# A packed attention followed by a squared-ReLU layer on one core: the first softmax in five token blocks instead of six, with a newly written order

## The chip, the core and the metric

The kernel runs on one core of a Trainium2 chip. The core has TensorE (PE; its weight loads are shown apart as PEld), VectorE (DVE), ScalarE (ACT), GpSimd (POOL) and SyncE (SP). Transfers are issued from POOL's, SP's and ACT's queues and are carried by 16 DMA engines. The metric is the time of one launch on the device, in microseconds (us). All other durations come from one profiled execution.

## The reference

Eight batches, eight heads, 576 tokens of 64 values, and 32 packing queries per head. Two attentions follow each other, and a two-layer network with a squared ReLU takes the result:

```python
def sm_attn(qq, kk, vv):
    s = scale * np.matmul(qq, kk.transpose(0, 1, 3, 2))
    s = s - np.max(s, axis=-1, keepdims=True)
    a = np.exp(s)
    a = a / (np.sum(a, axis=-1, keepdims=True) + 1e-09)
    return np.matmul(a, vv)
p_packed = sm_attn(p, k, v)              # 32 x 576 scores per head
out = sm_attn(q, p_packed, p_packed)     # 576 x 32 scores per head
x = out.transpose(0, 2, 1, 3).reshape(4608, 512)
h = np.maximum(x @ w_in, 0.0)            # w_in 512 x 2048
return (h * h) @ w_out                   # w_out 2048 x 512
```

## The kernel before

A batch is worked in two quads of four heads, so that 4 heads x 32 packing queries fill 128 partitions. Everything is done in bf16 with f32 accumulation; the POOL queue's loads cast on the way. The order of the work is a written string, `ORDER`, of some 2,000 words. Each word issues one step, each engine runs its own steps in the order of the words, and no scheduler moves them. A suffix names the engine: `:v` DVE, `:a` ACT, `:p` POOL; without one the engine is DVE. The digits after the letters are the batch and, where there is one, the quad. The words that matter here:

- `Lk`, `Lv`, `Lq`, `LA`, `LB`: loads of k and v (per quad), of q (per batch), and of the first 320 (A) and the other 256 (B) tokens of q in batches 0 and 1. `Wi` and `Wo` load pieces of w_in and w_out. They all go through POOL's one queue in the order of the words. `Pr`, `pg` load p, `Pu` makes a second copy of it with the partition halves swapped.
- First softmax: `kT` (DVE transposes k in 32x32 blocks, line 344), `s1` (scores, line 369), `m1` (maximum, line 393), `x1` (exponential on ACT, line 399), `eT` (PE transposes the result, line 412, in six blocks of 96 tokens), `eo` (copy out of PSUM), `pv` (times v, line 434: 6 blocks x 4 heads x 2 quads = 48 matmuls of 64 columns), `pp`, `bd`, `pt`, `po` (scaling and layouts of the packed result).
- Second softmax: `qT` or `qA`, `qB` (transposes of q, line 357), `s2` or `zA`, `zB` (scores), `t2`/`tA`/`tB`, `m2`/`mA`/`mB`, `sb`/`sA`/`sB`, `x2`/`xA`/`xB`, `su`/`uA`/`uB`, `a2`/`aA`/`aB` (back to rows, maximum, difference, exponential, sums, division) and `aT`/`TA`/`TB` (the result transposed, line 535).
- The packed result is multiplied with w_in first, so that the output of the second softmax needs no matmul of its own: `wa`, `wb`, `w0`, `w1` (line 546) and their copies `Wa`, `Wb`, `W0`, `W1` out of PSUM. `wa` and `wb` take the first half of the columns, in two parts; `w1` takes the second half.
- `h` (line 562) is the first layer: two matmuls for one of 16 blocks of 128 hidden columns and one part of the tokens. Blocks 0 to 3 and 8 to 11 need only `Wa` and `Wb`, the other eight need `W1`. `h0.0.*` are the 320 tokens of part A, `h0.1.*` the 256 of part B. `r` is the ReLU out of PSUM (ACT line 567, DVE line 569), `q` the square (lines 605, 607). Four PSUM banks take `h`, so an `h` waits for the `r` of four blocks before.
- `o` (line 618) is two of 16 matmuls of a tile of 128 output tokens, `c` its copy out of PSUM, `d` its store (line 639). The last tile is copied half by ACT (line 625) and half by DVE (line 626), and stored by two queues with two transfers each.
- `Z` (line 328) are idle matmuls that keep PE's clock up in the first 21 us.

## Time and profile before

| | us |
|---|---|
| median of three runs | 245.67 (244.76 to 246.89) |
| the profiled execution's own time | 245.67 |
| its span, first to last instruction | 243.9 |
| what lies around the span | 1.8 |
| PE busy | 231.7 |
| DVE busy | 205.9 |
| ACT busy | 142.4 |
| POOL busy | 69.3 |

The granted TensorE clock is 0.998 over the span. The profile's page gives the busy time of each engine, the span in 40 slices, the chain of work that ended last, and the costliest groups of instructions with their mean duration and the idle time before them. Durations in a group are those of one instruction; neighbours on PE overlap, so the pace of a group is read from the start of the first to the end of the last. "Idle before" with an arrow names what ended the wait.

### The profile page before, as it was taken

To read this page: it belongs to the slowest core of one execution; us is meant where nothing else is said; L and a number is where in the kernel's file an instruction comes from. 1 tells how busy PE (TensorE), PEld (TensorE's weight loads), DVE (VectorE), ACT (ScalarE), POOL (GpSimd) and SP (SyncE) were. 2 spreads that over 40 slices of the span, in tenths; PEclk is the share of its full clock that TensorE was granted. 3 is DMA by queue.
4 is the path that set the end of the run, shared out by engine and by line. 5 is a ranking of instruction groups with operands and counts; after the bars stand their busy time and mean duration, and the time that the engine had idled before them with its cause. 6 is when DMAs were issued, how large, how long until landed. Compare 5 with 4: busy or idle time off the path is not lost.

```text
span 243.9 us, 6139 instructions
## 1 busy us (share of the span) xinstructions
PE 231.7 (95%) x2424; PEld 128.8 (53%) x2460; DVE 205.9 (84%) x448; ACT 142.4 (58%) x315; POOL 69.3 (28%) x109
## 2 busy tenths in 40 slices
PE   8889899999999999999999999999999999999991
PEld 5556563455545655456445555565445554555540
DVE  3579987999989989798999999978898999677720
ACT  3418993577787859673666578644775667331200
POOL 8448832667690752072001800001000000000000
PEclk9999999999999999999999999999999999999999
DMA  6999999999999999456733991211332112121313
GB/s 152 198 197 209 203 207 200 143 192 273 161 193 212 168 154 217 86 74 115 111 73 82 121 173 27 63 43 46 50 90 59 36 38 46 43 60 28 86 43 86
DMA packets 34876, 29.00 MB, mean 119 GB/s; under 512 B 14112, under 2 KB 29856, under 8 KB 34848
## 3 DMA queue, kind: packets, MB, share of 16 engines
q0 software_dynamic: 28048, 18.26, 53.5%
q1 hardware_dynamic: 6640, 10.23, 16.0%
q8 instruction: 19, 0.31, 0.5%
q10 hardware_dynamic: 160, 0.13, 0.2%
q14 instruction: 9, 0.07, 0.1%
HBM read 37.22 MB, written 9.44 MB: 191 GB/s over the span
## 4 chain that ended last, share of the span: by engine, by line
PE 80%; DVE 9%; DMA 5%; issue 2%; POOL 1%; ACT 1%; POOLq 0%; ACTq 0%
PE ps_o L618 47%; PE ps_h L562 24%; DMA q_b<-in_q_dram 4%; PE ps_wp L546 3%; PE ps_s L369 3%; PE ps_e1T L412 2%; PE ps_pv L434 1%; DVE mx L500 1%; DVE gT L607 1%; DMA out_dram<-o_sb 1%; DVE sums L518 1%; DVE qT L357 1%; DVE r L569 1%; DVE s L495 1%; DVE s L492 1%
## 5 line engine op out<-in xcount | busy, mean ns | idle before, releaser
L618 PE MATMUL ps_o<-w_out_bf,gT 128*128 128x512 bf16 x540 | 145.1, 379 | 3.1 <-issue 1.7
L567 ACT ACTIVATE r<-ps_h 128x288 bf16<-128x288 f32 (+2 forms) x177 | 68.2, 417 | 51.9 <-PE ps_h L562 50.2
L562 PE MATMUL ps_h<-a2T,wp 128*128 128x288 bf16 (+2 forms) x512 | 91.2, 286 | 0.9 <-DVE wp L407 0.6
L618 PEld LDWEIGHTS <-gT 128*128 128x128 bf16 x576 | 53.7, 98 | 41.3 <-issue 5.5
L562 PEld LDWEIGHTS <-wp 128*128 128x128 bf16 x512 | 48.4, 98 | 44.1 <-issue 5.0
L607 DVE TENSOR_TENSOR gT<-r 128x576 bf16<-128x576 bf16 (+2 forms) x110 | 47.1, 445 | 2.6 <-ACT r L567 1.6
L569 DVE TENSOR_SCALAR r<-ps_h 128x288 bf16<-128x288 f32 (+2 forms) x79 | 34.9, 450 | 9.5 <-PE ps_h L562 8.9
L264 POOL DMA_DIRECT2D k_b<-in_k_dram x27 | 17.7, 656 | 47.3 <-DVE kT L344 37.2
L405 ACT CAST wp<-ps_wp 128x1024 bf16<-128x1024 f32 (+1 forms) x25 | 23.4, 953 | 6.1 <-PE ps_wp L546 6.1
L289 POOL DMA_DIRECT2D v_b<-in_v_dram x16 | 11.1, 697 | 39.8 <-PE ps_pv L434 38.0
L405 ACT COPY o_sb<-ps_o 128x512 f32<-128x512 f32 x25 | 14.5, 589 | 7.8 <-PE ps_o L618 7.6
L344 DVE STREAM_TRANSPOSE kT<-k_b 128x576 uint32<-128x576 uint32 x16 | 15.1, 950 | 2.4 <-DMA k_b<-in_k_dram 1.6
L399 ACT ACTIVATE e<-ps_s,nm 128x576 bf16<-128x576 f32 x16 | 11.8, 746 | 6.6 <-DVE nm L393 6.5
L328 PE MATMUL ps_idle<-gT 128*128 128x288 bf16 x92 | 14.5, 309 | 1.1 <-DVE gT L187 1.1
L512 ACT ACTIVATE e<-d 128x576 f32<-128x576 f32 (+2 forms) x20 | 11.4, 592 | 5.8 <-POOL d L506 4.0
L357 DVE STREAM_TRANSPOSE qT<-q_b 128x576 uint32<-128x576 uint32 (+2 forms) x20 | 12.2, 636 | 1.8 <-DMA q_b<-in_q_dram 1.6
L266 POOL DMA_DIRECT2D k_b<-in_k_dram x19 | 11.7, 617 | 3.8 <-DMA w_out_bf<-in_moe_w_out_dram 2.0
L407 DVE CAST wp<-ps_wp 128x1024 bf16<-128x1024 f32 x9 | 11.0, 1221 | 1.6 <-PE ps_wp L546 1.6
L518 DVE TENSOR_REDUCE sums<-e 128x18 f32<-128x576 f32 (+2 forms) x20 | 12.2, 612 | 0.0
L526 DVE TENSOR_TENSOR a<-e,rs 128x576 bf16<-128x576 f32 (+2 forms) x18 | 12.0, 680 | 0.0
L264 POOL DMA_DIRECT2D q_b<-in_q_dram x16 | 10.9, 684 | 3.3 <-DVE qT L357 2.3
L393 DVE TENSOR_REDUCE nm<-ps_s 128x1 f32<-128x576 f32 x16 | 11.6, 739 | 0.2 <-PE ps_s L369 0.2
(54 smaller groups left out, 179.2 us busy)
## 6 DMA issues: line engine op xcount, KB each, us to landing
out_dram<-o_sb SPq DMA_DIRECT2D x70, 128.0 KB, 2.4
v_b<-in_v_dram POOLq DMA_DIRECT2D x16, 288.0 KB, 7.4
w_out_bf<-in_moe_w_out_dram POOLq DMA_DIRECT2D x4, 512.0 KB, 12.5
q_b<-in_q_dram POOLq DMA_DIRECT2D x6, 288.0 KB, 7.5
q_b<-in_q_dram POOLq DMA_DIRECT2D x12, 144.0 KB, 7.5
k_b<-in_k_dram POOLq DMA_DIRECT2D x12, 108.0 KB, 4.5
w_in_bf<-in_moe_w_in_dram POOLq DMA_DIRECT2D x4, 256.0 KB, 11.3
w_in_bf<-in_moe_w_in_dram POOLq DMA_DIRECT2D x2, 512.0 KB, 13.0
```

The lines of the kernel that those rows point to most:

```text
L264: engine.dma_start(x[n:], s[:P - n])
L328: self.nc.tensor.matmul(ps[:, :HALF], lhsT=self.nought[:, :P], rhs=self.nought, start=True, stop=True)
L344: return self.nc.vector.transpose(t["kT"][:].rearrange("p (j l a) e -> p a j l e", j=J, a=3).bitcast(U32).rearrange("p a j l e -> p a j (l ...
L357: self.nc.vector.transpose(out.bitcast(U32), x.bitcast(U32))
L405: engine.copy(out, x)
L518: nc.vector.reduce_sum(out=sums[:, x], in_=t["e2"][:, x], axis=AX.X)
L526: engine.tensor_tensor(out=a2[:, y].rearrange("p t i e -> p t e i"), in0=t["e2"][:, x].rearrange("p (t e) i -> p t e i", e=2), in1=t["rs"] ...
L562: self.nc.tensor.matmul(ps, lhsT=t["wp"][:, fb // n, fb % n * P:(fb % n + 1) * P], rhs=t["a2T"][:, s0:s1], start=(qd == 0), stop=(qd == se ...
L567: engine.activation(r, ps, ACT.Relu)
L569: engine.tensor_scalar_max(r, ps, 0.0)
L607: engine.tensor_tensor(out=out, in0=r, in1=r, op=ALU.mult)
L618: self.nc.tensor.matmul(self.o[tt], lhsT=self.gT[:, fb, a:a + P], rhs=self.w_out_bf[:, fb, :], start=(i == 0), stop=(i == self.NFB - 1))
```

## The change

Five edits and a new order:

- From batch 2 on, the first softmax is transposed in four blocks of 128 tokens (every fourth token, so the weights of the transpose are read at a step of 4 elements) and a fifth block that holds the last 128 tokens again, of which v has the first 64 rows set to zero. So `eT` has 5 transposes for 6 and `pv` 40 matmuls for 48. Batches 0 and 1 keep six blocks of 96, read at a step of 6.
- v goes to static tiles: in batches 0 and 1 into parts of the big tile `gT` that are not yet used, from batch 2 into three tiles in turn, with two transfers for each instead of one.
- The keys are transposed in token order, so that `kT` writes without a step, and k comes in runs of nine tokens instead of three from batch 2. The exponential puts the columns in order instead: it writes each row of bf16 at a step of 18 elements.
- The last output tile is copied into two tiles, each stored by one transfer; the tokens of its block are laid out so that each transfer takes 128 rows. The last `aT` becomes two transposes.
- The second p load is issued from ACT's queue, not SP's; `Pu` is two copies by an engine, not two transfers.
- `ORDER` is another one from the start to the end. Idle matmuls: 90 instead of 92.

The start of the order is shown, and every changed function; the rest of `ORDER` is cut.

```diff
 NP = 32
-J = 6
 T = 18
-PS = 96
-S = J * PS
+S = T * NP
 HALF = S // 2
...
+THREES = range(2)
+
 PIECES = range(2)
...
 ORDER = """
-Lk00 I pf Lk01 Lv00 LB0 Lv01 kc:v kc:a LA0 pg P0 Wi11 kT00 Wi01 Wi00 kT01 Z32 s100 Wi10 Z1 s101 m100 Wi21 m101 x100
-x101 qB01 Wi20 Z10 eT00 qB00 eo00:a Z1 eT01 rd0 eo01:v Lk10 Z4 pv0 pp0 Z4 pt0 bd0 Lk11 qA01 po0:a zB0 qA00 tB00 Z2 zA0
-P1 tA01 tA00 mA01 mA00 sA01:p mB00 Lv10 sA00:v xA01 tB01 xA00 sB00:p uA01 Z23 wa01 wa00 Wo0 uA00 Wa00:a Wa01:a aA01:v
-mB01 xB00 aA00:p Z8 wb01 wb00 TA01 Wb01:a Lv11 sB01:v Wb00:a TA00 uB00 xB01 Z7 h0.0.0 h0.0.2 uB01 r0.0.0:a aB00:p
-h0.0.3 h0.0.9 r0.0.2:a Wo2 h0.0.8 aB01:v h0.0.10 r0.0.3:a TB00 r0.0.9:v r0.0.8:a h0.0.1 TB01 h0.0.11 q0.0.4:a
-r0.0.10:v h0.1.2 q0.0.1:p r0.0.1:v h0.1.8 r0.0.11:a r0.1.2:v h0.1.1 q0.0.0:a r0.1.8:v h0.1.9 h0.1.0 r0.1.9:a LA1
-q0.0.5:v w101 r0.1.1:a w100 q0.1.4:v W101:a h0.1.10 W100:v h0.1.3 h0.1.11 LB1 r0.1.0:a r0.1.3:a kT10 q0.1.0:p h0.0.12
-r0.1.10:a r0.1.11:a h0.1.7 h0.1.14 q0.1.1:a r0.0.12:v h0.0.13 Wo1 r0.1.14:a kT11 h0.1.12 r0.1.7:a h0.0.4 q0.1.5:a
+Lk00 I pf Lk01 Lv00 Lv01 LA0 kc:v kc:a Wi01 P0 kT00 Wi00 LB0 Z30 s100 Wi10 kT01 Wi11 m100 Z4 s101 Wi21 m101 x100 x101
+Wi20 Z15 eT00 rd0 eT01 eo00:v pg eo01:v Lk10 qA01 Z5 pv0 qA00 pp0 Lk11 Z4 pt0 bd0 zA0 po0:v tA01 tA00 Z4 wa01 mA01
+Wa01:a Z1 wa00 mA00 Wa00:a sA01:p qB01 Wo0 sA00:v xA01 qB00 xA00 uA01 Lv10 Z13 zB0 uA00 aA01:p tB00 Lv11 aA00:v Z8
+wb00 mB00 Wb00:a TA01 sB00:p TA00 tB01 Z6 h0.0.9 P1 h0.0.8 xB00 h0.0.0 mB01 r0.0.8:a uB00 wb01 sB01:p r0.0.0:a h0.0.1
+Wb01:a r0.0.9:v LA1 xB01 r0.0.1:v h0.0.10 aB00:p q0.0.4:a h0.0.3 uB01 h0.0.2 h0.0.11 q0.0.0:v r0.0.10:a r0.0.3:a
+r0.0.2:v aB01:p r0.0.11:a TB00 q0.0.1:v w100 Wo2 w101 TB01 W100:a q0.0.5:v h0.1.8 h0.1.9 W101:v h0.1.1 r0.1.9:a h0.1.0
+LB1 r0.1.8:a h0.1.3 r0.1.0:a h0.1.2 q0.1.4:v r0.1.1:a h0.0.4 r0.1.3:a kT10 q0.1.0:p h0.0.5 r0.1.2:a h0.0.13 r0.0.4:a
+kT11 h0.0.6 r0.0.5:a h0.0.12 Wo1 r0.0.13:a q0.1.1:v h0.0.7 r0.0.6:a q0.0.2:v s11 r0.0.12:a Wo3 h0.1.4 r0.0.7:v
+q0.0.6:a h0.1.15 m110 h0.1.12 q0.0.3:p r0.1.4:a h0.0.15 r0.1.12:a h0.1.14 r0.1.15:v r0.0.15:a h0.1.6 m111 h0.1.13
...
 """
...
         self.att, self.den, self.r, self.o, self.o_sb, self.ph = {}, {}, {}, {}, {}, {}
-        self.stage, self.open = -1, {}
+        self.stage, self.open, self.loaded_v = -1, {}, 0
         self.engines = {"v": self.nc.vector, "a": self.nc.scalar, "p": self.nc.gpsimd}
...
         nc.vector.memset(self.nought, 0.0)
+
+        self.v_b = [self.consts.tile([P, QH, 5, D], BF16, name=f"v_b{i}") for i in range(3)]
+        for x in self.v_b:
+            nc.vector.memset(x[:P // 2, :, 4, :], 0.0)
...
             self.load_rows(self.p_f[:, self.NQ + qd, :],
-                           self.p[1, qd * QH:qd * QH + QH].rearrange("h i d -> (h i) d"), qd, self.nc.sync)
+                           self.p[1, qd * QH:qd * QH + QH].rearrange("h i d -> (h i) d"), qd, self.nc.scalar)
...
-    def p_rest(self, word):
+    def p_rest(self, word, engine):
...
         else:
-            self.nc.sync.dma_start(z[P // 2:], y[:P // 2])
-            self.nc.sync.dma_start(z[:P // 2], y[P // 2:])
+            self.copy(engine, z[P // 2:], y[:P // 2])
+            self.copy(engine, z[:P // 2], y[P // 2:])
...
         if n == "v":
-            x = t[n] = self.ld.tile([PS, QH, J, D], BF16, name="v_b")
-            self.nc.gpsimd.dma_start(x, s.rearrange("h (p j) d -> p h j d", j=J))
+            self.load_v(t, s, b, qd)
             return
         x = t[n] = self.ld.tile([P, T, D], BF16, name="k_b")
+        s = s.rearrange("h (l t) d -> (h l) t d", t=T)
         if b == 0 and qd == 0:
-            self.nc.sync.dma_start(self.k_f, s.rearrange("h (l t) d -> (h l) (t d)", t=T))
+            self.nc.sync.dma_start(self.k_f, s.rearrange("p t d -> p (t d)"))
+        elif b in WIDE:
+            for hf, y in enumerate(WIDE_CUTS):
+                self.load_rows(x[:, y, :], s[:, y, :], qd + 2 * hf)
+        else:
+            self.load_rows(x, s, qd if b else 0)
+
+    def load_v(self, t, s, b, qd):
+
+        if b in THREES:
+            c = b * S
+            x = self.gT[:, self.NFB - 2 - 2 * b - qd, c:c + QH * 6 * D].rearrange("p (h j d) -> p h j d", h=QH, d=D)[:S // 6]
+            t["v"] = [x[:, :, j, :] for j in range(6)]
+            self.nc.gpsimd.dma_start(x, s.rearrange("h (p j) d -> p h j d", j=6))
             return
-        s = s.rearrange("h (l t) d -> (h l) t d", t=T)
-        if b in WIDE:
-            for hf in range(2):
-                y = slice(hf * J // 2, (hf + 1) * J // 2)
-                self.load_rows(*(z.rearrange("p (a j) d -> p a j d", j=J)[:, :, y, :] for z in (x[:], s)), qd + 2 * hf)
-        else:
-            self.load_rows(x, s, qd if b else 0)
+        x = self.v_b[self.loaded_v % len(self.v_b)]
+        self.loaded_v += 1
+        t["v"] = [x[:, :, j, :] for j in range(5)]
+        self.nc.gpsimd.dma_start(x[:, :, :4, :], s[:, :4 * P].rearrange("h (p j) d -> p h j d", j=4))
+        self.nc.gpsimd.dma_start(x[P // 2:, :, 4, :], s[:, 4 * P:].rearrange("h p d -> p h d"))
...
         t["kT"] = self.tp.tile([P, S, 2], BF16, name="kT")
-        return self.nc.vector.transpose(
-            t["kT"][:].rearrange("p (j l a) e -> p a j l e", j=J, a=3).bitcast(U32).rearrange("p a j l e -> p a j (l e)"),
-            t["k"][:].rearrange("p (a j) d -> p a j d", j=J).bitcast(U32))
+        self.nc.vector.transpose(t["kT"][:].rearrange("p s e -> p (s e)").bitcast(U32),
+                                 t["k"][:].rearrange("p t d -> p (t d)").bitcast(U32))
...
             self.den[b] = self.sm.tile([P, 2], F32, name="den")
-        self.nc.scalar.activation(e1[:].rearrange("p (a s) -> p a s", a=2), t["ps_s1"][:, :, :HALF], ACT.Exp,
+        self.nc.scalar.activation(e1[:].rearrange("p (l a u) -> p a u l", a=2, u=T // 2),
+                                  t["ps_s1"][:, :, :HALF].rearrange("p a (u l) -> p a u l", l=NP), ACT.Exp,
                                   bias=t["nm"], accum_out=self.den[b][:, qd:qd + 1])
...
     def st_e1T(self, t, b):
-        ps = self.bank16(b, "ps_e1T")[:PS, :J * P].rearrange("p (j c) -> p j c", c=P)
-        for j in range(J):
-            self.nc.tensor.transpose(ps[:, j, :], t["e1"][:, j * PS:(j + 1) * PS], self.ident)
+
+        m = 6 if b in THREES else 4
+        n = S // m // NP
+        n = min(n, QH)
+        x = [t["e1"][:, j:n * m * NP:m] for j in range(m)]
+        if n * m < T:
+            x.append(t["e1"][:, S - P:])
+        ps = self.bank16(b, "ps_e1T")[:n * NP, :len(x) * P].rearrange("p (j c) -> p j c", c=P)
+        for j, y in enumerate(x):
+            self.nc.tensor.transpose(ps[:, j, :], y, self.ident)
         t["ps_e1T"] = ps
     def st_e1T_out(self, t, engine):
-        t["e1T"] = self.tp.tile([PS, J, P], BF16, name="e1T")
-        self.copy(engine, t["e1T"], t["ps_e1T"])
+        ps = t["ps_e1T"]
+        t["e1T"] = self.tp.tile([P, T // 3, P], BF16, name="e1T")[:ps.shape[0], :ps.shape[1], :]
+        self.copy(engine, t["e1T"], ps)
...
         n = len(qds)
-        for j, i in [(j, i) for j in range(J) for i in range(n)] if b else [(j, i) for i in range(n) for j in range(J)]:
+        m = range(len(self.att[b, qds[0]]["v"]))
+        for j, i in [(j, i) for j in m for i in range(n)] if b else [(j, i) for i in range(n) for j in m]:
             t = self.att[b, qds[i]]
...
                 self.nc.tensor.matmul(ps[g:g + NP, i, :D], lhsT=t["e1T"][:, j, g:g + NP],
-                                      rhs=t["v"][:, h, j, :], start=(j == 0), stop=(j == J - 1))
+                                      rhs=t["v"][j][:, h, :], start=(j == 0), stop=(j == m[-1]))
...
-    def st_a2T(self, t, hf=None):
+    def st_a2T(self, t, hf=None, last=False):
...
         a2T = self.new(t, self.keep, "a2T", [P, S], BF16)
-        self.nc.vector.transpose(a2T[:, x.start * NP:x.stop * NP].bitcast(U32),
-                                 t["a2"][:, x.start // 2:x.stop // 2].rearrange("p t i e -> p (t i e)").bitcast(U32))
+        y = slice(x.start // 2, x.stop // 2)
+        if last:
+            y = slice(y.start, y.stop - 2)
+            self.nc.vector.transpose(a2T[:, y.stop * 2 * NP:].bitcast(U32).rearrange("p (l t) -> p t l", t=2),
+                                     t["a2"][:, y.stop:].rearrange("p t i e -> p t (i e)").bitcast(U32))
+        self.nc.vector.transpose(a2T[:, y.start * 2 * NP:y.stop * 2 * NP].bitcast(U32),
+                                 t["a2"][:, y].rearrange("p t i e -> p (t i e)").bitcast(U32))
...
     def step_c(self, engine, tt):
-        o = self.o_sb[tt] = self.op.tile([P, self.NE], F32, name="o_sb")
         ps, h = self.o.pop(tt), self.NE // 2
         if tt == self.B * S // P - 1:
-            self.nc.scalar.copy(o[:, :h], ps[:, :h])
-            self.nc.vector.tensor_copy(o[:, h:], ps[:, h:])
-        else:
+            o = self.o_sb[tt] = [self.op.tile([P, self.NE], F32, name="o_sb")[:, :h] for _ in range(2)]
+            self.nc.scalar.copy(o[0], ps[:, :h])
+            self.nc.vector.tensor_copy(o[1], ps[:, h:])
+        else:
+            o = self.o_sb[tt] = self.op.tile([P, self.NE], F32, name="o_sb")
             self.copy(engine, o, ps)
     def step_d(self, engine, tt):
-        nc = self.nc
-        o, h = self.o_sb.pop(tt), self.NE // 2
-        for n in range(P // (2 * NP)):
-            bl, cc = divmod(tt * P + n * 2 * NP, S)
-            rows = self.out[bl * S:(bl + 1) * S, :].rearrange("(l t e) n -> t l e n", t=T // 2, e=2)[cc // (2 * NP)]
-            src = o[n * 2 * NP:(n + 1) * 2 * NP]
-            last = tt == self.B * S // P - 1
-            for eng, c in ((nc.scalar, slice(0, h)), (nc.sync, slice(h, 2 * h))) if last else ((nc.sync, slice(0, 2 * h)),):
-                eng.dma_start(rows[:, :, c], src[:, c])
+
+        o, h, m = self.o_sb.pop(tt), self.NE // 2, 2 * NP
+        rows = self.out.rearrange("(b l t e) n -> b t l e n", b=self.B, t=T // 2, e=2)
+        if tt == self.B * S // P - 1:
+            rows = self.out[-S:].rearrange("(l t) n -> l t n", t=T)[:, T - 4:]
+            self.nc.scalar.dma_start(rows[:, :, :h], o[0])
+            self.nc.sync.dma_start(rows[:, :, h:], o[1])
+            return
+        for n in range(2):
+            b, t = divmod(tt * 2 + n, T // 2)
+            self.nc.sync.dma_start(rows[b, t], o[n * m:n * m + m])
...
             "a2": lambda: self.st_a2(t, engine),
-            "aT": lambda: self.st_a2T(t),
+            "aT": lambda: self.st_a2T(t, last=b == self.B - 1),
             "tA": lambda: self.st_turn2(t, 0),
...
         elif word in ("Pr", "Px", "Pt", "Pu"):
-            self.p_rest(word)
+            self.p_rest(word, engine)
         elif word[:2] == "kc":
```

151 lines of the change are left out of this document (75 added, 76 removed).

## The prediction

> **What bounds the kernel now.** The page's busy times and its chain of work come first.
>
> ```profile
> PE 231.7 (95%) x2424; PEld 128.8 (53%) x2460; DVE 205.9 (84%) x448; ACT 142.4 (58%) x315; POOL 69.3 (28%) x109
> ...
> PE 80%; DVE 9%; DMA 5%; issue 2%; POOL 1%; ACT 1%; POOLq 0%; ACTq 0%
> ```
>
> PE holds four fifths of the chain. The table of windows (us, PE busy, PEld, DVE, ACT, POOL, PE's clock, DMA share, GB/s) tells where it is not busy:
>
> ```profile
> 25.00:30.00 5.00, 4.34 (x73) 2.48 (x70) 4.92 (x9) 5.00 (x15) 4.20 (x6) 1.00 1.23 202
> 30.00:35.00 5.00, 4.89 (x83) 3.16 (x73) 5.00 (x13) 4.91 (x14) 1.94 (x3) 1.00 1.26 207
> ...
> 120.00:130.00 10.00, 9.79 (x106) 4.43 (x101) 9.93 (x18) 6.90 (x16) 0.00 (x0) 1.00 0.24 54
> ```
>
> From about 36 to 239 us PE is full: the nineteen 10 us windows from 40 to 230 leave it 2.9 us idle in all. DVE is nearly as full (9.93 of 10), so the order keeps both. Between 25 and 35 us ACT and DVE are full and PE is not, and before 21.4 us PE does mostly idle matmuls. So an edit is worth what it takes from PE after 36 us, what it moves of the moment from which PE is full, and what it takes from the end. The timeline of the start, all engines:
>
> ```profile
> 14.38 0.91 DVE L357 STREAM_TRANSPOSE qT<-q_b 128x320 uint32<-128x320 uint32 x2 [0.82 <-DMA q_b<-in_q_dram]
> ...
> 21.44 4.02 PE L562 MATMUL ps_h<-a2T,wp 128*128 128x320 bf16 x26
> ...
> 23.53 0.29 DVE L535 STREAM_TRANSPOSE a2T<-a 128x128 uint32<-128x128 uint32 x1
> ...
> 25.40 0.63 PE L546 MATMUL ps_wp<-w_in_bf,ppT 64*32 64x512 bf16 x16
> ...
> 27.40 2.10 PE L562 MATMUL ps_h<-a2T,wp 128*128 128x320 bf16 x14 [0.61 <-DVE wp L407]
> ...
> 33.44 0.50 PE L412 MATMUL ps_e1T<-ident,e 128*96 128x128 bf16 x6
> ...
> 34.73 0.56 PE L434 MATMUL ps_pv<-v_b,e1T 96*32 96x64 bf16 x48
> ```
>
> Part A of batch 0 waits for its q, which lands at 14.36 us (part B's q at 10.90); `h` begins at 21.44, part B is ready at 23.8, and `w1` starts at 25.40, when the last piece of w_in has landed (issued at 11.19, 14.1 us to landing: 25.3).
>
> **The change part by part: PE.** Six transposes of 219 ns take 0.50 us, so each further one (0.50 - 0.22)/5 = 56 ns; two fewer per batch, 0.11. 48 `pv` matmuls of 193 ns take 0.56, so (0.56 - 0.19)/47 = 8 ns each; eight fewer, 0.06. Six batches: **-1.05 us**, all in the full stretch. The loads of the transposes' weights now step 4 or 6 elements. The nearest rows are weights at a step of 2 (pT, 88 ns for 32 columns) and of 1 (ppT, 89): no cost, which I take. Above, a doubled pace of 56 ns x 84 transposes = +4.7; below nothing, as the pace is the 128 streamed columns.
>
> **DVE and ACT.** kT becomes as cheap as qT:
>
> ```profile
> L344 DVE STREAM_TRANSPOSE kT<-k_b 128x576 uint32<-128x576 uint32 x16 | 15.1, 950 | 2.4 <-DMA k_b<-in_k_dram 1.6 <-PE ps_s L369 0.6
> L357 DVE STREAM_TRANSPOSE qT<-q_b 128x576 uint32<-128x576 uint32 x12 | 9.0, 759 | 0.2
> ```
>
> 16 x 0.19 = 3.1 us of DVE. The new order spends it: counted through both programs with the rows' means, DVE gets six more `r` of 288 (2.7), three fewer of 320 (-1.4), one more W (1.2), two fewer `c` (-1.4), two copies for `Pu` (about 0.9, estimated from the 0.46 of k's cast of 576 columns), zeroing of v (0.5 in the first 2 us, under the wait for k at 4.26) and +1.3 of small moves: +0.7 net, while ACT loses about 5. DVE stays as full as it was, so in the middle the edit is worth at most those 2.9 idle us of PE; I take 0. The exponential (746 ns) now writes at a step of 36 bytes, which no row shows. The nearest is kT above, which writes at 12 bytes: +25%, +0.19 us, which I take; bounds 0 and twice the time (+0.75). After 36 us ACT's idle 42% hides it; at the start see below.
>
> **Transfers.** v costs POOL twelve issues more (0.7 us each); POOL is 28% busy, and queued behind them are only later loads. k from batch 2 moves in runs three times as long. Both land far ahead of use: 0 (bounds -0.3 and +1, a late v at one `pv`). p goes from SP to ACT behind the second exponential, three issues of 0.5, where ACT waits anyway. SP loses two transfers of pT.
>
> **The start.** POOL's loads land one after the other. Moving LB from third to seventh lets A's q land LB's 1.26 (10.90 - 9.64) earlier, at 13.1. The seventh load lands one w_in quarter (1.27) ahead of the eighth, whose set of bytes is the old one (18.1): LB at 16.85. The rest is DVE's queue. From 13.1: two qA 0.91, pp 0.42, bd 0.24, 0.6 through `zA`, two tA 0.87, two mA 0.91: 17.1; then in the written order qB 0.41, sA 0.48, qB 0.41, two uA 1.32, tB 0.42, aA 0.46, mB 0.41, two TA 0.66: **21.7**. So `h` starts 0.3 later than at 21.44, although A's q is earlier. Between the last TA and the last TB DVE now has tB, p's scaling and turn, mB, uB, r, r, uB, q, r, TB, q, TB = 0.42 + 0.43 + 0.41 + 0.6 + 0.95 + 0.6 + 0.49 + 0.48 + 0.3 + 0.49 + 0.3 = 5.5: part B is ready at **27.2**, before at 23.8. PE has for this time 8 words of part A (2.2 us), wb01 (0.4) and, once the last w_in lands at 25.3, `w1` (0.65). It stands from 25.95 to 27.2, with 16 matmuls of `h` done where the old kernel had 32: 16 x 0.109 = 1.75, less the 0.4 of waiting it had itself at 27.4, is 1.35 behind at least.
>
> Then PE waits for `r`. From W100 to s11 the new order gives ACT eleven `r` in a row and DVE none (W101, three squares, two kT). Rows of ACT show 2.18 us for six: 0.37 each. The first can start at 27.65; s11 stands behind h0.0.7, which needs the bank of the eighth: 27.65 + 8 x 0.37 = 30.6, and kT ends at 30.8. s11 at 30.9 against 29.43, with 40 matmuls of `h` ahead instead of 46 (6 x 0.122 = 0.73): 2.2 behind. Up to the first `eT` ACT has three more `r`, a square (0.7), four `r` and the exponential (0.95): 31.75 + 0.7 + 1.5 + 0.75 = 34.7, before 32.37, with two matmuls fewer: **2.6 behind**. From there `o` fills PE. The two exponentials of batch 1 lie on this chain: 0.2 of their 0.4. Start: **+2.8**, bounds +1.35 and +4.
>
> **The end.** The last copies:
>
> ```profile
> 239.01 0.37 ACT L625 COPY o_sb<-ps_o 128x256 f32<-128x256 f32 x1 [10.62 <-PE ps_o L618]
> 239.42 1.29 ACTq L639 DMA_DIRECT2D out_dram<-o_sb  x2
> 239.42 0.42 DVE L626 COPY o_sb<-ps_o 128x256 f32<-128x256 f32 x1 [2.35 <-DMA out_dram<-o_sb]
> 239.87 1.18 SPq L639 DMA_DIRECT2D out_dram<-o_sb  x2
> ```
>
> DVE's half starts as ACT's ends (239.38). In the changed program, too, DVE's copy waits for ACT's, both read one PSUM tile; I count nothing for two SBUF tiles. One issue instead of two saves SP 0.6, a store of 128 KB lands up to 0.35 later than one of 64 (2.4 and 2.05): **-0.4**, bounds -1.0 (the copies do overlap) and 0.
>
> **Sum.** +2.8 - 1.05 - 0.4 = +1.35 on this execution's 245.67 (243.9 span and 1.8 around it), which is the median of the runs: **247.0**. A measurement of this kernel tells about 1% (2.5 us) from no change.
>
> **Rivals.** (1) *The hole closes* (16%): DVE and PE catch up because ACT's queue is not as full as counted. For it: the old kernel had 0.6 waits there, too. Against: the string of eleven `r`. Start 0: 245.67 - 1.45 = 244.2. (2) *And the middle gains* (6%): kT's freed 3 us take half of PE's idle 2.9, and the copies overlap at the end: 244.2 - 1.5 - 0.6 = 242.1, faster. (3) *The strided exponential* (16%), the slower side: ACT writes 2 bytes at 36, and if that doubles its time, x110 and x111 put 1.5 us, not 0.2, into the stretch where ACT is last: 248.3, and with 0.2 us at each later batch where `eT` stands directly behind it, 249.5. It decides from +0.7 us per exponential. Beside it: the Trainium skill, SBUF — State Buffer, section "Door 1: The DMA port swizzle", says that SBUF serves 16-byte lines, that an access which moves to a new line each time pays, and that bf16 can step 8 elements for free. By that the new writes pay and the transposes' reads at 4 and 6 do not; kT's 12-byte step, which costs 25% here, is within the free range by that rule, so the trace agrees with it in kind only. (4) *The weights' steps double a transpose* (7%): +4.7, 251.7. Speaks against it: pT's 88 ns.
>
> **Chances.** The forecast, 55%, reaches from 245.6 (start +1.35) to 248.2 (+4). Range 243.6 to 250.0: it takes in (1) and (3) and leaves out (2), (4) and part of the forecast's tails. Faster by over 1% (under 243.2): (2) and a little of (1), 0.09. Slower by over 1% (over 248.1): (3), (4) and the forecast's upper end, 0.33. Same: 0.58.
>
> **What will show it.** Right: first `h` near 21.7, a PE wait for TB or for `r` near 26 to 27, s11 near 31, first `eT` of batch 1 near 34.7, kT at 760, pv at 0.50, DVE's last copy still behind ACT's. Wrong: first `h` before 20.5, s11 before 30, exponentials over 1.3 us, six transposes over 0.7 us, or waits of PE after 40 us that add up to over 4 us.

## The result, and the profile after

The changed kernel takes 274.37 us (median of four runs, 272.24 to 276.65), against 245.84 before: 1.113 times as long, with an interval of 1.105 to 1.122. The prediction was 247.0, from 243.6 to 250.0. It was wrong by 27 us. The ratios leave out executions that were slower at a lower granted clock, here the one of 276.65 us (0.963) and, in the run below with the step on the read, its profiled one (303.04 us at 0.756). The profiled execution has 274.54 us of its own and a span of 272.8. The page's busy times, the chain and the slices of ACT and of PE's clock:

```profile
PE 245.6 (90%) x2398; PEld 131.6 (48%) x2398; DVE 206.2 (76%) x459; ACT 165.6 (61%) x308; POOL 74.9 (27%) x124
...
ACT  2616993569487493869885535986287856533400
...
PEclk9979997999799995999999999999999999999999
...
PE 73%; ACT 13%; issue 6%; DMA 3%; DVE 3%; ACTq 0%; SPq 0%; POOL 0%; POOLq 0%
```

DVE has the same work as before (206.2 us). ACT has 23 us more and holds 13% of the chain, before 1%. The clock, a row of nines before, has four dips. The groups and the waits name the place:

```profile
L413 ACT ACTIVATE e<-ps_s,nm 128x576 bf16<-128x576 f32 x16 | 42.4, 2801 | 3.9 <-DVE nm L407 3.9
...
L434 PE MATMUL ps_e1T<-ident,e 128*128 128x128 bf16 (+1 forms) x84 | 10.0, 264 | 14.9 <-ACT e L413 14.9
...
...
L445 DVE RECIPROCAL rden<-den 128x2 f32<-128x2 f32 x8 | 1.3, 164 | 15.2 <-ACT e L413 15.2
```

The strided exponential takes 2801 ns instead of 746. PE waits 14.9 us for it ahead of the transposes `eT`, and DVE 15.2 us ahead of the reciprocal of its sums; before, neither the matmuls of `eT` nor the reciprocal waited for ACT (only the weight loads of `eT` did, for 0.6 us in all). kT came down to 756 ns, as was forecast. The timeline at batch 1, where the two exponentials stand one behind the other:

```profile
34.91 2.74 ACT L413 ACTIVATE e<-ps_s,nm 128x576 bf16<-128x576 f32 x1
37.16 2.96 ACT L413 ACTIVATE e<-ps_s,nm 128x576 bf16<-128x576 f32 x1
37.71 1.01 PE L434 MATMUL ps_e1T<-ident,e 128*96 128x128 bf16 x6 [1.66 <-ACT e L413]
39.62 0.51 ACT L413 ACTIVATION_READ_ACCUMULATOR e<-ps_s,nm 128x1 f32 x1
40.18 1.06 PE L434 MATMUL ps_e1T<-ident,e 128*96 128x128 bf16 x6 [1.03 <-ACT e L413]
```

The read of the accumulated sum behind each one has grown too, from 0.21 to 0.50 us. Waits also come without `eT`, since everything else on ACT stands behind the exponential:

```profile
126.62 2.75 ACT L413 ACTIVATE e<-ps_s,nm 128x576 bf16<-128x576 f32 x1
...
128.87 0.74 ACT L596 ACTIVATE r<-ps_h 128x288 bf16<-128x288 f32 x1
...
129.66 0.40 PE L591 MATMUL ps_h<-a2T,wp 128*128 128x288 bf16 x2 [1.32 <-ACT r L596]
```

Here PE waits 1.32 us for a ReLU that could start only behind the exponential and its sum. So the theory is: the whole loss is the exponential's writing at a step of 36 bytes (Theory 1). The rival: the new order and the stepped transposes lose a large part, and the exponential is only where the waits show.

### The profile page after: what moved, and what is told of

Its sections match the earlier page's. It is cut to its first block, busy times and chain, and to the rows that moved or that the text cites. A ratio compares the mean times of both kernels' runs of the same rounds, so it can differ in the third digit from the quotient of the medians.

```text
span 272.8 us, 6063 instructions
## 1 busy us (share of the span) xinstructions
PE 245.6 (90%) x2398; PEld 131.6 (48%) x2398; DVE 206.2 (76%) x459; ACT 165.6 (61%) x308; POOL 74.9 (27%) x124
## 4 chain that ended last, share of the span: by engine, by line
PE 73%; ACT 13%; issue 6%; DMA 3%; DVE 3%; ACTq 0%; SPq 0%; POOL 0%; POOLq 0%
PE ps_o L647 41%; PE ps_h L591 21%; ACT e L413 10%; PE ps_wp L575 3%; PE ps_s L383 3%; ACT r L596 2%; PE ps_e1T L434 2%; DMA k_b<-in_k_dram 2%; PE ps_pv L458 1%; PE ps_idle L343 1%; DMA out_dram<-o_sb 1%; DVE sums L542 0%; ACT wp L420 0%; PE ps_ppT L497 0%; DVE a2T L564 0%
## 5 line engine op out<-in xcount | busy, mean ns | idle before, releaser
L647 PE MATMUL ps_o<-w_out_bf,gT 128*128 128x512 bf16 x576 | 152.3, 386 | 0.0
L647 PEld LDWEIGHTS <-gT 128*128 128x128 bf16 x576 | 55.4, 99 | 46.7 <-issue 7.4
L413 ACT ACTIVATE e<-ps_s,nm 128x576 bf16<-128x576 f32 x16 | 42.4, 2801 | 3.9 <-DVE nm L407 3.9
L434 PE MATMUL ps_e1T<-ident,e 128*128 128x128 bf16 (+1 forms) x84 | 10.0, 264 | 14.9 <-ACT e L413 14.9
L315 POOL DMA_DIRECT2D v_b<-in_v_dram x12 | 9.3, 779 | 48.5 <-PE ps_pv L458 48.5
L268 POOL DMA_DIRECT2D k_b<-in_k_dram x27 | 14.8, 557 | 22.6 <-DVE kT L359 17.7
L268 POOL DMA_DIRECT2D q_b<-in_q_dram x16 | 10.9, 692 | 29.2 <-DVE qT L371 29.2
L343 PE MATMUL ps_idle<-gT 128*128 128x288 bf16 x90 | 16.2, 338 | 1.1 <-DVE gT L187 1.1
L434 PEld LDWEIGHTS <-e 128*128 128x128 bf16 (+1 forms) x84 | 8.0, 150 | 18.7 <-ACT e L413 18.0
L359 DVE STREAM_TRANSPOSE kT<-k_b 128x576 uint32<-128x576 uint32 x16 | 11.8, 756 | 1.4 <-DMA k_b<-in_k_dram 1.3
L445 DVE RECIPROCAL rden<-den 128x2 f32<-128x2 f32 x8 | 1.3, 164 | 15.2 <-ACT e L413 15.2
L343 PEld LDWEIGHTS <-gT 128*128 128x128 bf16 x90 | 9.5, 114 | 6.2 <-issue 1.4
```

Of the source, the lines that this page charges most:

```text
L268: engine.dma_start(x[n:], s[:P - n])
L343: self.nc.tensor.matmul(ps[:, :HALF], lhsT=self.nought[:, :P], rhs=self.nought, start=True, stop=True)
L413: self.nc.scalar.activation(e1[:].rearrange("p (l a u) -> p a u l", a=2, u=T // 2), t["ps_s1"][:, :, :HALF].rearrange("p a (u l) -> p a u ...
L434: self.nc.tensor.transpose(ps[:, j, :], y, self.ident)
L647: self.nc.tensor.matmul(self.o[tt], lhsT=self.gT[:, fb, a:a + P], rhs=self.w_out_bf[:, fb, :], start=(i == 0), stop=(i == self.NFB - 1))
```

## The experiments

### The exponential without its step

```diff
-        self.nc.scalar.activation(e1[:].rearrange("p (l a u) -> p a u l", a=2, u=T // 2),
-                                  t["ps_s1"][:, :, :HALF].rearrange("p a (u l) -> p a u l", l=NP), ACT.Exp,
+        self.nc.scalar.activation(e1[:].rearrange("p (a s) -> p a s", a=2), t["ps_s1"][:, :, :HALF], ACT.Exp,
```

> The changed kernel, but the first exponential writes its row without a step, in the order in which the scores come. The columns then stand for other tokens than the transposes and v take them for, so the order of the tokens is left out of the first softmax; every instruction stays, in number and size. Theory 1, the strided write: the 28.5 us come from the sixteen first exponentials, 2.80 us and 0.50 for the sum instead of 0.75 and 0.21, and from PE standing for them (14.9 us) and running at a lower clock after it. Then the exponential is back at 0.75 and the time at 245 to 249 (the recorded sum without the exponential's share is 246.8). Rival, the rest of the change (new order, weights at steps of 4 and 6, v in two transfers): the exponential falls, but the time stays above 262.

245.96 us, ratio 0.998 [0.995, 1.000]. The whole loss is gone.

```profile
PE 235.5 (97%) x2398; PEld 129.2 (53%) x2398; DVE 205.6 (84%) x459; ACT 137.9 (57%) x308; POOL 75.1 (31%) x124
...
L413 ACT ACTIVATE e<-ps_s,nm 128x576 bf16<-128x576 f32 x16 | 11.8, 745 | 4.8 <-DVE nm L407 4.7
```

This run is also the trace on which the other steps of the prediction can be read, free of the exponential; the next section does that. Against it the changed kernel is 29.2 us of span longer: PE's idle time rose from 8.1 to 27.2 us (+19.1), its busy time from 235.5 to 245.6 (+10.1, most of it matmuls at half clock: the record shows 17.1 us at half, which is worth 8.5).

### The step alone, in the old order

The same two lines of code the other way round, in the kernel before:

```diff
-        self.nc.scalar.activation(e1[:].rearrange("p (a s) -> p a s", a=2), t["ps_s1"][:, :, :HALF], ACT.Exp,
+        self.nc.scalar.activation(e1[:].rearrange("p (l a u) -> p a u l", a=2, u=T // 2),
+                                  t["ps_s1"][:, :, :HALF].rearrange("p a (u l) -> p a u l", l=NP), ACT.Exp,
```

> The kernel before, with the changed kernel's strided write in the first exponential and nothing else of it (the order of the tokens is left out of the first softmax). Theory 1: the exponential takes 2.8 us here, too, so it comes from the write and not from what runs beside it; ACT gets 16 x 2.35 = 37.6 us more work, and the time rises to between 262 and 280. Rival (the new order makes it slow, by contention with what now runs at the same time): under 1.5 us each, and the time stays under 252.

274.76 us in one execution, 28 us above the kernel before. The same line carries it:

```profile
L399 ACT ACTIVATE e<-ps_s,nm 128x576 bf16<-128x576 f32 x16 | 42.5, 2804 | 6.9 <-DVE nm L393 6.9
L413 PE MATMUL ps_e1T<-ident,e 128*96 128x128 bf16 x96 | 9.0, 235 | 13.5 <-ACT e L399 13.5
...
196.78 0.41 PE L563 MATMUL ps_h<-a2T,wp 128*128 128x288 bf16 x2 [1.61 <-ACT r L568]
```

Neither the new order nor the five blocks are needed for the loss: Theory 1 stands, from both sides.

### The same order of columns, with the step on the read

```diff
-        self.nc.scalar.activation(e1[:].rearrange("p (l a u) -> p a u l", a=2, u=T // 2),
-                                  t["ps_s1"][:, :, :HALF].rearrange("p a (u l) -> p a u l", l=NP), ACT.Exp,
+        self.nc.scalar.activation(e1[:].rearrange("p (l a u) -> p l a u", a=2, u=T // 2),
+                                  t["ps_s1"][:, :, :HALF].rearrange("p a (u l) -> p l a u", l=NP), ACT.Exp,
```

> The changed kernel with all it computes, but the step of the first exponential stands on its read from PSUM (32 columns of 4 bytes apart, 128 bytes, in runs of one) and its write goes through the row in order. If the price is that of SBUF writes of 2 bytes in new lines, the exponential takes 0.75 to 0.95 us and the time is 245 to 250. If any step costs ACT the same, on whichever side, it takes over 2 us and the time stays above 265.

246.13 us, ratio 0.999 [0.996, 1.001], and the exponential takes 742 ns (744 and 745 in the three later runs that keep this read from batch 2 on): reading f32 from PSUM at 128 bytes' step costs nothing. The loss was not in permuting, but in the side on which it was done.

### A table of steps

The kernel before, with another step at each place: the first exponential writes at 16 steps, the second at 12, kT at six, and the transposes read their weights at six. The columns only change places for the sake of the step, so token order is left out.

> The kernel before as a table of steps (the order of the values within a row is left out, so the result is not the reference's): the sixteen first exponentials write bf16 at a step of 1, 2, 3, 4, 6, 8, 9, 12, 16, 18, 24, 32, 36, 48, 72 and 144 elements, the twelve second ones of batches 2 to 7 write f32 at 1 to 36, kT writes 4-byte elements at 1, 2, 3, 6, 9 and 18, and the first transposes read their 96 weight columns at 1 to 6. Theory A, a line of 16 bytes: bf16 writes grow up to a step of 8 and stay flat from there, f32 writes up to 4, kT up to 4; weights at 1, 2 and 4 keep the pace of 56 ns, at 6 they take 133 as in batch 0 of the changed kernel. Theory B, any step costs alike: 2 is as dear as 18. Theory C, it is the number of bytes apart (or a bank that 36 bytes hits): it goes on growing beyond 16, or single steps stand out.

The timeline of ACT, the first exponential's writes of 2 bytes at steps of 1, 4, 8 and 18 elements:

```profile
10.00 0.74 ACT L403 ACTIVATE e<-ps_s,nm 128x576 bf16<-128x576 f32 x1 [5.01 <-DVE nm L396]
...
33.45 1.57 ACT L403 ACTIVATE e<-ps_s,nm 128x576 bf16<-128x576 f32 x1
...
62.46 2.91 ACT L403 ACTIVATE e<-ps_s,nm 128x576 bf16<-128x576 f32 x1
...
113.70 2.77 ACT L403 ACTIVATE e<-ps_s,nm 128x576 bf16<-128x576 f32 x1
```

| step in elements | 1 | 2 | 3 | 4 | 6 | 8 | 18 | 36 |
|---|---|---|---|---|---|---|---|---|
| first exponential, bf16, ns | 741 | 902 | 1237 | 1572 | 2181 | 2908 | 2767 | 2752 |
| second exponential, f32, ns | 714 | 754 | 1002 | 1262 | 1271 | 1248 | 1270 | 1317 |
| kT, 4 bytes, DVE, ns | 736 to 769 | 742 to 779 | 932 to 968 | | 1182 to 1203 | | 1239 to 1250 | |
| one transpose, 96 columns of weights, ns | 56 | 56 | 67 | 90 | 133 | | | |

From a step of 2 to one of 8 the bf16 row is within 60 ns of 230 + 335 x step, and beyond it is flat (2.7 to 3.1 us up to a step of 144). That fits a cost for every 16-byte line that the write comes to, until each element has its own. The 2908 at a step of 8 holds some 0.2 us more than a free-standing one, as it runs directly behind another exponential; in the changed kernel such a one takes 2.94 to 2.96 us and one by itself 2.72 to 2.75. The f32 row is flat from a step of 4 elements on, also 16 bytes (1198 to 1317 ns up to 36, and one of 1631 at 24), and kT from 6 on at the latest, but both much lower: an element in a line of its own takes about 2.2 ns with 4 bytes (1248 / 576) and 4.8 to 5.0 ns with 2 (2767 and 2908 / 576). Whether the size of the element alone makes that difference is not shown: the first exponential also reads from PSUM and adds up a sum, the second reads from SBUF and does not. kT at 12 bytes, the row on which the prediction rested, sits on the slope of the cheaper curve.

### A step of four

```diff
-        self.nc.scalar.activation(e1[:].rearrange("p (l a u) -> p a u l", a=2, u=T // 2),
-                                  t["ps_s1"][:, :, :HALF].rearrange("p a (u l) -> p a u l", l=NP), ACT.Exp,
+        self.nc.scalar.activation(e1[:].rearrange("p (x a g) -> p a g x", a=2, g=2),
+                                  t["ps_s1"][:, :, :HALF].rearrange("p a (g x) -> p a g x", g=2), ACT.Exp,
```

> The changed kernel with the first exponential written at a step of 4 elements (8 bytes) instead of 18; the table of steps gave 1572 ns for it, so it takes about 0.83 us more than an unstepped one, which is the size that rival (3) of the prediction priced. Left out: the token order of the first softmax (the columns come out in another order than v's). Theory 1, rival (3)'s sum is right and only the size of the exponential was wrong (2.8 us and not 1.5): 246.0 (the changed order with an unstepped exponential) + 1.3 to 2.5 = 247.3 to 248.5, PE idle after 36 us under 3 us, the clock record whole. Theory 2, a wait of PE on the exponential costs more than itself since the clock falls after it: above 250, with half-clock stretches in the record. Transposes at 6 and 4 columns' step as in the changed kernel, in both.

250.23 us, ratio 1.018 [1.015, 1.021]: about 5 us more than without a step. Theory 1's sum fails, and Theory 2's reason fails too: the clock is whole.

```profile
PEclk9999999999999999999999999999999999999999
...
L413 ACT ACTIVATE e<-ps_s,nm 128x576 bf16<-128x576 f32 x16 | 23.7, 1550 | 4.8 <-DVE nm L407 4.8
```

What the price is, the start of each batch's first transposes shows (us, from the timelines):

| batch | 1 | 2 | 3 | 4 | 5 | 6 | 7 | end of span |
|---|---|---|---|---|---|---|---|---|
| no step | 33.08 | 56.57 | 87.22 | 106.50 | 128.16 | 161.42 | 187.06 | 243.6 |
| step of 4 | 33.54 | 57.56 | 89.90 | 109.65 | 132.47 | 166.12 | 192.10 | 248.7 |
| step of 18 | 37.71 | 65.36 | 102.70 | 126.28 | 151.77 | 187.81 | 216.13 | 272.8 |

The step of 18 loses 4.2 us with a batch on average (2.7 to 6.7) and never gets any back; the step of 4 loses 0.7 (0.3 to 1.7). An exponential with its sum takes 0.83 us without a step, 1.55 at 4 and 2.72 to 2.97 at 18. Where the two of a batch stand one behind the other, as in batches 1 and 2, the pair takes 1.55, 2.88 and 5.2 us from start to end, so it is 1.3 or 3.7 us longer. In the run without a step, `eT` starts 0.13 to 1.5 us behind the end of its exponential in batches 1 to 4; that much of a longer one is hidden there. And a late `eT` is no cover by itself: in batch 5 it starts 15 and 20 us behind the exponentials of 18 elements' step, and still PE waits 1.58 us for an `r` queued behind one of them (at 137.06) and 0.81 us ahead of `pt` (at 140.59). So at 4 about half of what the pair gains in length is hidden, and at 18 nothing: there the loss is a little more than the pair gains, and it holds the half clock of the next part.

### The clock

In the changed kernel the clock record shows half speed from 16.4 to 19.8, 40.3 to 43.7, 67.6 to 71.0 and 101.7 to 108.5 us, each time behind 3.4 us in which PE had been busy for only 0.7 to 2.1. Transposes of the identity were put ahead of seven groups of `eT`:

```diff
+WARM = {(1, 0): 24, (1, 1): 14, (2, 0): 18, (2, 1): 26, (3, 0): 44, (4, 0): 18, (7, 0): 36}
...
+        for _ in range(WARM.get((b, qd), 0)):
+            self.nc.tensor.transpose(ps[:, 0, :], self.ident[:, :n * NP], self.ident)
         for j, y in enumerate(x):
             self.nc.tensor.transpose(ps[:, j, :], y, self.ident)
```

> The changed kernel as it is, with transposes of the identity put ahead of the seven groups of eT for which PE waited longest (24, 14, 18, 26, 44, 18 and 36 of them at 56 ns, 1.0 to 2.5 us each, all shorter than the wait that they fill). They take PE no time that it had to use; they only keep it busy while it waits for the strided exponential. In the changed kernel's profile the clock is at half for 3.4, 3.4 and 6.8 us after such waits at 38, 65 and 100 us. Theory 1, the half clock follows from PE standing idle: those three stretches go, and with them about 13.7 / 2 = 6.8 us: 266 to 269. Theory 2, the clock falls for another reason (power, the long exponentials themselves): the stretches stay, 274 or more. If PE's waits only grow by what the clock gives back, since ACT sets the pace there, it lies between: 270 to 273 with a whole clock record after 20 us.

271.45 us, ratio 1.100 [1.096, 1.104]. The clock record of the profiled execution (272.94, the slowest of the four), PE's waits for the exponential ahead of the added transposes (L435; us in all, times, longest), and the first group with the `eT` behind it:

```profile
PEclk9959999999999999999999999999999999999999
...
PE ps_e1T L435 <- ACT e L414: 5.8, 5, 1.7
...
39.27 1.50 PE L435 MATMUL ps_e1T<-ident 128*96 128x128 bf16 x24 [1.66 <-ACT e L414]
40.61 0.96 PE L437 MATMUL ps_e1T<-ident,e 128*96 128x128 bf16 x6
```

After 21.4 us the clock is whole, with exponentials as long as before, so the half clock did go with PE's idle time, and Theory 2 falls; the time lies where the third case had it, between 270 and 273. (Ahead of it, at the start, where nothing was added, it is at half from 14.5 to 21.4 us.) But the added transposes did not only fill waits. They write into the PSUM tile of `eT`, which takes its place in turn with the score tiles that the exponential reads, and in four of the seven groups they themselves stood until that group's exponential had ended, as at 39.27 us, where its end is at 39.22; in a fifth they began 0.15 us behind it. There they come on top of the wait and hold `eT` up, by 5.5 us in all; only in batches 3 and 7 do they lie inside the wait. From the start of batch 1's first exponential to the end it is 234.7 us against 237.9, so 3.2 us come back in spite of that, of the 6.8 that the three later stretches are worth, and 2.9 us by the medians. What the half clock costs is therefore only bounded: at least the 2.9 us that came back, a tenth of the loss, and at most the 8.5 that 17.1 us at half speed are worth.

### Is DVE the bound? Two tests

The prediction took DVE's freed 3 us at nothing. First kT without a step in the kernel before:

```diff
-        return self.nc.vector.transpose(
-            t["kT"][:].rearrange("p (j l a) e -> p a j l e", j=J, a=3).bitcast(U32).rearrange("p a j l e -> p a j (l e)"),
-            t["k"][:].rearrange("p (a j) d -> p a j d", j=J).bitcast(U32))
+        return self.nc.vector.transpose(t["kT"][:].rearrange("p s e -> p (s e)").bitcast(U32),
+                                        t["k"][:].rearrange("p t d -> p (t d)").bitcast(U32))
```

> The kernel before with one edit: the keys are transposed without a step, so kT takes 0.76 instead of 0.95 us, 16 times: 3.0 us less of DVE. Left out: the pairing of tokens with v in the first softmax. It measures what I took at nothing in the prediction (DVE's 3 us in the middle). Theory 1, PE is full from 36 us on and DVE's freed time is worth nothing but the start, where three kT lie on DVE's queue ahead of the second softmax: -0.2 to -0.6, ratio 0.9975 to 0.999. Theory 2, the order keeps DVE and PE even, so half of PE's 2.9 us of idle time go: -1.5 to -2, ratio 0.992 to 0.994.

kT takes 760 ns, and the time is 245.71, ratio 1.000 [0.998, 1.001]: nothing, Theory 1. Then the other way, with the step of 72 bytes on kT in the changed kernel and a plain exponential:

```diff
-        self.nc.vector.transpose(t["kT"][:].rearrange("p s e -> p (s e)").bitcast(U32),
-                                 t["k"][:].rearrange("p t d -> p (t d)").bitcast(U32))
+        self.nc.vector.transpose(
+            t["kT"][:].rearrange("p (l t) e -> p t l e", t=T).bitcast(U32).rearrange("p t l e -> p t (l e)"),
+            t["k"][:].bitcast(U32))
```

> The whole change, with the token order made by DVE's kT (4-byte elements written 72 bytes apart, 1.24 us by the table of steps, against 0.76) and not by the exponential, which is plain (0.75). So the same step sits on 4-byte writes of DVE instead of 2-byte writes of ACT: 16 x 0.48 = 7.7 us more of DVE and 16 x 2.05 = 33 us less of ACT. Theory 1, DVE is as full as PE: nearly all of the 7.7 us comes out, 251 to 254. Theory 2, DVE has slack after 36 us where the order lets it run ahead: 246.5 to 249, of which 1 to 2 us lie before 36 us.

```profile
L359 DVE STREAM_TRANSPOSE kT<-k_b 128x576 uint32<-128x576 uint32 x16 | 19.3, 1244 | 2.0 <-DMA k_b<-in_k_dram 1.1
```

249.53, ratio 1.014 [1.011, 1.017], about 4 us above the run without any step (3.3 by the spans): half of the 7.8 us added, between the two theories and a little above the second one's 249. So, in these two orders, DVE's time is worth nothing when taken away and half of itself when added: PE is the bound, and DVE is near it.

### What the rest of the change is worth

With the step on the read, the old order's words up to `po1` were put ahead of the new order's rest, and batches 0 and 1 got their old layout (kT at 12 bytes, plain exponential, transposes without a step).

> The whole change with the step on the exponential's read (as in the run before with the step in the read), and two things put back: the words of the old order up to po1 (the copy of batch 1's packed result), and in batches 0 and 1 the old layout, in which kT writes at 12 bytes, the exponential is plain and the six transposes read their weights without a step. From batch 2 on the new five blocks and the new order. Theory 1, the start had cost 0.7 us in the new order (first transposes of batch 1 at 33.08 against 32.37) and the transposes at a step of 6 cost batch 1 2 x 6 x (133 - 56) ns = 0.9: 246.0 - 1.6 = 244.4, ratio to before about 0.992, the gain of the five blocks (-1.05) and of the end seen for the first time. Theory 2, DVE is as full as PE, so what PE saves comes back as waits for DVE: 245.5 to 246.5, ratio 0.997 to 1.0.

246.96, ratio 1.003 [1.001, 1.006]: 0.3% slower, against both theories. The timeline of DVE shows why:

```profile
18.16 0.23 DVE L225 TENSOR_SCALAR p_b<-gT 128x128 bf16<-128x128 f32 x1 [3.18 <-DMA gT<-in_p_dram]
```

`P1` scales batch 1's p. ACT issues that load behind the second exponential, from 10.26 us, and it lands at 18.03; in the old order's place `P1` holds up the second softmax of batch 0. That wait belongs to this mix of two orders and not to the change, whose own order has `P1` later. Moved there:

> The run before (old order's words up to po1, old layout of batches 0 and 1, the rest of the change, the step in the exponential's read) with one word moved: P1, DVE's scaling of batch 1's p, stands ahead of the first h instead of ahead of the second softmax's first turn. There DVE had waited 3.18 us for p, whose transfers ACT now issues only behind the second exponential (at 10.3 to 11.2 us, landed at 18.0); the first transposes of batch 1 stood at 34.98 us, 2.6 behind the kernel before, while the span was only 0.6 longer. Theory 1, the rest of the change is worth 2.0 us and the start alone lost it: the first transposes at 32.4, span 241.9, time 243.7, ratio 0.988 to 0.993. Theory 2, the later start was hidden by waits that come back: 245 to 246, ratio 0.996 to 1.0.

245.48, ratio 0.995 [0.993, 0.998]: the first version with all of the reference's work that is clear of the kernel before, by half a percent; it is the number of Theory 2. The first `eT` of batch 1 stands at 32.15 us as expected, that of batch 2 at 54.64, 1.9 us ahead of the run without a step; then one wait takes it all:

```profile
60.74 1.44 DVE L376 STREAM_TRANSPOSE qT<-q_b 128x576 uint32<-128x576 uint32 x2 [2.10 <-DMA q_b<-in_q_dram]
...
62.54 0.63 PE L586 MATMUL ps_wp<-w_in_bf,ppT 64*32 64x512 bf16 x16 [1.82 <-DVE ppT L431]
```

The q of batch 2 landed at 60.62. With `qT` moved behind what PE waited for:

```diff
-pp2 h1.0.11 qT21 q1.0.7:a h1.0.10 Lv30 o6.4 qT20 r1.0.11:a pt2
+pp2 h1.0.11 q1.0.7:a h1.0.10 Lv30 o6.4 r1.0.11:a pt2
...
-q1.0.6:a r1.1.2:v w121 r1.1.5:a w120 W121:v
+q1.0.6:a r1.1.2:v qT21 qT20 w121 r1.1.5:a w120 W121:v
```

> The run before with qT21 and qT20 (DVE's transposes of batch 2's q) moved from behind pp2 to behind r1.1.2. In the run before, PE reached the first transposes of batch 2 at 54.6 us, 1.9 earlier than in the changed order with a plain exponential (56.57), and lost just that in one wait of 1.82 at 62.54: DVE stood 2.10 us at qT for batch 2's q, whose last transfer landed at 60.62, with bd2 and the copy of the packed result queued behind it. Theory 1, only the place in DVE's queue cost it: without qT ahead bd2 runs at 58.6, qT at 61.6 when q has landed, and the 1.8 us stay gained to the end: span 241.8, time 243.7, ratio 0.986 to 0.991. Theory 2, loads as a whole set the pace there (190 GB/s from 40 to 60 us), so the next transfer is late in turn, kT or s2 of batch 3 waits, and it stays at 245 to 246, ratio 0.994 to 0.998.

245.18, ratio 0.996 [0.994, 0.999]: not told apart from the run before. The wait of 1.82 is gone and `s2` waits 0.52 in its place. The start was 0.8 us slower in this execution (first `eT` of batch 1 at 32.91). Over the run without a step the lead is 1.2 us at the first `eT` of batch 2 (55.40) and 0.3 at that of batch 3 (86.90 against 87.22); PE stands idle for 0.9 us between the two, in the run without a step for none. The number is Theory 2's again, but its reason is not shown: neither PE nor DVE waits for a transfer from 55 to 87 us, and what makes up the idle time beyond those 0.52 is not settled. With a step that costs nothing and the old start, the whole change is worth about 1 us.

## Why the prediction was wrong

**The step that failed** is in the part on DVE and ACT: "The nearest is kT above, which writes at 12 bytes: +25%, +0.19 us, which I take; bounds 0 and twice the time (+0.75)." It measured +2.06, and +0.29 in the read of the sum. Three things were wrong in it. kT's row was one point below the knee, on another engine and with elements of 4 bytes; the table has 2767 at this step. The upper bound of twice the time had no row behind it, so the range did not hold the bounds of the unknown cost. And what was asked of the trace was ACT's average: "After 36 us ACT's idle 42% hides it". What hides a longer exponential is the time between its end and the start of its `eT`, and the time for which PE can go on without the ReLUs queued behind it. The first could be read ahead of any run, in the trace of before:

```profile
32.09 0.22 ACT L399 ACTIVATION_READ_ACCUMULATOR e<-ps_s,nm 128x1 f32 x1
32.37 0.54 PE L412 MATMUL ps_e1T<-ident,e 128*96 128x128 bf16 x6
32.81 0.23 ACT L399 ACTIVATION_READ_ACCUMULATOR e<-ps_s,nm 128x1 f32 x1
```

With the second `eT` of batch 1 at 33.44 us, it is 0.05 and 0.41 us in batch 1, 0.98 and 0.81 in batch 2, 1.09 and 2.00 in batch 3, 0.43 and 0.11 in batch 5. With 1.9 us a piece more, or 3.7 where the two stand one behind the other, batch 1 alone loses 3.3 and batch 2 2.8. The second shows only in the runs: with the step alone in the old order, PE waits 1.61 us at 196.8 for an `r` behind an exponential whose `eT` is 17 us away.

**Rival (3)** named the mechanism, the slower side and even the sign by which to know it (exponentials over 1.3 us, waits of PE after 40 us over 4 us), but at 2 x and not 3.8 x the time, and for the start alone with 0.2 us a later batch. The step of four tests that size: exponentials of 1550 ns cost 5 us, where it had 1.3 to 2.5. Its own working was too small by half or more, since it too put the waits of the later batches at almost nothing (0.2 us each).

What the rival cites of the Trainium skill (SBUF — State Buffer, section "Door 1: The DMA port swizzle") can now be held against the table. The 16 bytes fit: both rows of ACT go flat there. That bf16 steps free up to 8 elements is not what ACT's writes did: 741 ns at 1, 902 at 2 and 2908 at 8. Nor was kT's step of 12 bytes, which by that rule is free: the prediction's "agrees with it in kind only" was too kind to the rule. The measurement decides.

**The other steps**, read on the run without a step (its span 243.6 against 243.9):

- *Start, +2.8, bounds +1.35 and +4.* Measured +0.7 (first `eT` of batch 1 at 33.08 against 32.37), below the bound. The first half came out: A's q landed at 12.99 (forecast 13.1), first `h` at 21.70 (21.7), the last of w_in at 25.20 (25.3). That `h` fits to the digit is luck: B's q landed at 17.74 and not at 16.85, DVE waited 0.73 us for it, and the steps from there to the last TA, counted at 4.57, took 3.87. The tail of DVE's queue did not come out:

```profile
17.77 0.45 DVE L371 STREAM_TRANSPOSE qT<-q_b 128x256 uint32<-128x256 uint32 x1 [0.73 <-DMA q_b<-in_q_dram]
...
21.70 0.99 PE L590 MATMUL ps_h<-a2T,wp 128*128 128x320 bf16 x6
...
25.97 0.30 DVE L563 STREAM_TRANSPOSE a2T<-a 128x128 uint32<-128x128 uint32 x1
26.32 3.43 PE L590 MATMUL ps_h<-a2T,wp 128*128 128x256 bf16 x23 [0.24 <-DVE a2T L563]
```

  Part B was ready at 26.27, not 27.2: the steps took 4.6 us from the last TA and not 5.5, mainly since neighbours on DVE overlap by some 0.07 us and the sum added whole durations. And the eleven `r` in a row took 3.42 us, 0.31 each; the 0.37 came from a row of six in 2.18 us, while a row of four beside it (1.22 us) had 0.31. So `s11` stood at 29.69 and not 30.9.
- *PE, -1.05.* In the rows the five blocks bring it (40 `pv` in 0.49 us for 48 in 0.56, five transposes at 56 ns for six), but the six blocks of batches 0 and 1, read at a step of 6, cost 133 ns a transpose instead of 56: 0.8 us in batch 1 (groups of 0.93 and 0.91 us, before 0.54 and 0.50). From the first `eT` of batch 1 to the last matmul it is 206.40 us against 206.56, so -0.16: by these rows the two nearly cancel. Rival (4) doubled all 84 transposes; only the 24 with 96 columns pay, and the 60 with 128 columns at a step of 4 keep 56. The Trainium skill, TensorE: Matmul & The Clock Gate, section "Weight-path perf modes — Fast Weight Load (FWL) and DoubleRow", has the fast load on for 128 weight columns, strided or not, which agrees with the 60.
- *The end, -0.4.* From the last matmul to the end of the span 4.13 us against 4.93, so -0.8, within the bounds; a little of it returns behind the span, where this run's ten executions have 1.74 to 2.36 us and those of the kernel before beside them 1.73 to 1.84. DVE's copy still waits for ACT's, which ends at 239.89, as forecast:

```profile
239.93 0.42 DVE L654 COPY o_sb<-ps_o 128x256 f32<-128x256 f32 x1 [3.17 <-ACT o_sb L653]
```

- *DVE's freed time, 0.* Right, measured alone.

Start, PE and end cover the whole span between them, so without the exponential the change comes to 0.7 - 0.16 - 0.8 = -0.3. Rival (1), the hole closes, was then nearest, but for the exponential.

## What to carry to other kernels

A write at a new step needs a row with the same engine and element size, and beyond the knee; where there is none, its upper bound is open and belongs in the range, and the step may be free on the other side of the instruction (here the read from PSUM). An operation in front of the bound engine is hidden by its slack, from its end to the start of its reader, batch by batch, and not by its engine's idle share. Where a loop repeats it, the part above the slack is paid every time.

## What was not expected of the hardware

- A bf16 write of ACT (576 columns) costs some 335 ns more per element of step, from 2 elements (902 ns) to 8, which are 16 bytes (2908), then stays at 2.7 to 3.1 us up to a step of 144; an f32 write stays at 1.2 to 1.3 from 4 elements on, but for one of 1.63.
- The read of the accumulated sum behind a strided exponential grows with it, from 193 to about 500 ns.
- ACT reads PSUM at a step of 128 bytes as fast as in order (742 to 745 against 745 ns).
- Weights of 96 columns slow a transpose from a step of 3 on (67, 90, 111 and 133 ns at 3, 4, 5 and 6); 128 columns at a step of 4 do not (56).
- The half clock came in stretches of 3.4 or 6.8 us. It followed where PE had been busy for 2.4 of 5 us (35 to 40), and did not follow a single wait of 1.46 us (126.28).
